# Second MoE of an attention + MoE + MoE kernel: token blocks of 256, 512, 512, 512 in place of seven of 256, and products of 512 and 384 columns

## The chip, the cores and the metric

One core of one Trainium2 chip runs the kernel. Times are device microseconds (us). The metric is the time of one execution. The kernel before took 1158.94 us in the median of 3 runs (1152.77 to 1166.38). A further execution was profiled, and the rows below come from it.

## The reference

Three stages run one after the other, all in float32:

```python
q_n, k_n = rmsnorm(q, g_q), rmsnorm(k, g_k)          # q, k, v: (4, 12, 448, 64)
attn = softmax(q_n @ k_n^T / 8);  x = attn @ v       # then to x: (1792 tokens, 768)
h = x @ w_in; s = h * softmax(h); x = (layernorm(s) * g_ln) @ w_out      # 768 -> 1024 -> 768
h = x @ w2_in; g = h - tanh(h);   out = g @ w2_out                       # 768 -> 2048 -> 768
```

The weights of both MoE stages come as 64-bit floats, and the kernel converts them on the chip.

## The kernel before

**Numbers.** Every operand of a product is split into a high part (float32r, what TensorE multiplies in one pass) and a low part (the remainder). A product of two split operands is three matmuls into the same PSUM buffer: high by high, high by low, low by high. That is `three` (L174 to L177), so the matmuls of all stages carry the lines L175, L176 and L177, and the tile names tell them apart. `split` (L179 to L181) makes a high part on ScalarE (L180) and the low part on VectorE (L181).

**Stages.** Attention runs over pairs of heads. The first MoE runs over four blocks of tokens (384, 384, 384 and 384+256), one block behind the attention that feeds it: `x_split` loads and splits tokens (tiles xr, xs), `moe_h` multiplies by w_in (hps), `layer_norm` works on the rows (hb), `moe_lnT` transposes them on TensorE (lps) and splits them (lnT), and `moe_x2` multiplies by w_out (x2ps), copies the result to SBUF (x2) and writes it to a DRAM buffer, x2d. The last block's `moe_h` and `moe_x2` run when attention is over.

**The second MoE** goes over 8 spans of 256 hidden columns, and in each span over the token blocks, 7 of 256. `h2(sp, i)` (L785) multiplies block i by the span's input weights: the weights stand still, 256 tokens move, 36 matmuls into one PSUM buffer h2ps (pool ps_h, 5 buffers). Tanh on ScalarE (L797), h - tanh(h) on VectorE (L798) and a split follow (tile gT, 2 buffers). `out2(sp, i)` (L803) takes gT as the standing operand and 256 columns of the output weights as the moving one: three PSUM buffers ops (pool ps_m, 3 buffers) of 12 matmuls, each then added by VectorE to the block's sum in SBUF, ob (L820; in the first span ScalarE copies it, L818). `out2` of a block is written after `h2` of the next.

**Tokens of the second MoE.** `x2_load(i)` (L775) reads block i back from x2d with one DMA and splits it in two halves (tiles x2s): two ScalarE instructions, then two VectorE ones. Blocks 0 and 1 are loaded before the first MoE's last block is finished, so that their `h2` can fill TensorE's waits there. The other five have buffers only when the first MoE's pools are closed (L836, L837).

**Weights of the second MoE.** `Stream.convert` (L116) turns one raw tile of 64-bit floats into a split weight: one GpSimd instruction (L131), four on VectorE (L132, L133, L137, L140), one on ScalarE (L153), one on GpSimd (L154). A span needs three tiles of w2_in (kind in2) and three of w2_out (out2). There are 4 buffers for them before the first MoE ends and 9 after.

**Order.** A scheduler puts each engine's instructions in a fixed order when the program is built, by its own cost estimates. Each engine then works through its list strictly in that order, and an instruction whose input is late holds up all behind it on that engine. All DMAs are issued by SyncE (SP), whose list is as strict.

Of the kernel before, what the change touches and what calls it, by code (L numbers as in the profile page):

```python
# [18 lines left out]
def kernel(  # L19
# [24 lines left out]
    TB = 256  # L44
    NB = NTOK // TB
# [49 lines left out]
    class Stream:  # L95
# [20 lines left out]
        def convert(self, kind, i, pool, save):  # L116
# [3 lines left out]
            w = pool.tile([128, 2, a, b], F32R, tag="w6", name="w6")  # L120
# [39 lines left out]
        def conv(self, n):  # L160
            while self.nc < min(n, len(self.items)):
                self.load(self.nc + 1)
                kind, i, again = self.items[self.nc]
                if again:
                    a, b = source(kind, i)[1]
                    w = self.pool().tile([128, 2, a, b], F32R, tag="w6", name="w6")
                    nc.sync.dma_start(out=w.bitcast(F32), in_=saved[kind, i])
                else:
                    w = self.convert(kind, i, self.pool(), self.save)
                self.got[self.nc] = w  # L170
                self.nc += 1
                self.load(self.nc + 2)
# [356 lines left out]
    Bp = {}  # L529
# [171 lines left out]
    ws = Stream(items, lambda: Bp["w"], True)  # L701
# [49 lines left out]
    def open_c(side, sizes):  # L751
        for name, bufs in sizes:
            C.setdefault(name, []).extend(
                [ec.enter_context(tc.tile_pool(name=f"c_{name}_{side}", bufs=bufs, side=side))] * bufs
            )

    CI, CW = 2, 4
    open_c("right", (("w", CW), ("xh", 2 * CI), ("ob", CI), ("g", 2), ("th", 2)))
# [3 lines left out]
    n_w = [0]  # L762

    def next_w():
        n_w[0] += 1
        return C["w"][(n_w[0] - 1) % len(C["w"])]
# [8 lines left out]
    def x2_load(i):  # L775
        x2 = C["ob"][i].tile([128, KD, TB], F32, tag="x", name="x2")
        nc.sync.dma_start(out=x2, in_=x2d[:, :, TB * i:TB * i + TB])
        pr = []
        for z in range(2):
            s = C["xh"][2 * i + z].tile([128, 2, 3, TB], F32R, tag="xh", name="x2s")  # L780
            split(s[:, 0], s[:, 1], x2[:, 3 * z:3 * z + 3])
            pr.append(s)
        xs_t.append(pr)

    def h2(sp, i):  # L785
        ps = ps_h.tile([128, 2, TB], F32, tag="h", name="h2ps")
# [16 lines left out]
    def out2(sp, i, G):  # L803
        if sp == 0:
            ob[i] = C["ob"][i].tile([128, 2, DM], F32, tag="x", name="ob")
        for th in range(DM // 256):
            ps = ps_m.tile([128, 2, 256], F32, tag="m", name="ops")
            for t in range(2):
                for f in range(2):
                    w = w2.got[6 * sp + 3 + th]  # L810
                    cols = slice(128 * t, 128 * t + 128)
                    three(
                        ps[:, t], (G[:, 0, f, cols], G[:, 1, f, cols]), (w[:, 0, f], w[:, 1, f]),
                        f == 0, f == 1,
                    )
            o = ob[i][:, :, 256 * th:256 * th + 256]
            if sp == 0:
                nc.scalar.activation(out=o, in_=ps, func=AF.Copy)  # L818
            else:
                nc.vector.tensor_tensor(out=o, in0=ps, in1=o, op=ALU.add)  # L820
            if sp == NSP - 1 and i == NB - 1:
                nc.sync.dma_start(
                    out=out[TB * i:TB * i + TB, 256 * th:256 * th + 256].rearrange("(t p) d -> p t d", p=128), in_=o
                )
        if sp == NSP - 1 and i < NB - 1:
            nc.sync.dma_start(
                out=out[TB * i:TB * i + TB, :].rearrange("(t p) d -> p t d", p=128), in_=ob[i]
            )

    w2.conv(CW)  # L830
    for i in range(CI):
        x2_load(i)
# [4 lines left out]
    open_c("left", (("w", 5), ("xh", 2 * (NB - CI)), ("ob", NB - CI)))  # L837
    prev = None
    for sp in range(NSP):
        for i in range(NB):  # L840
            if sp == 0 and i >= CI:
# [44 lines left out]
```

## Time and profile before

| what | value |
|---|---|
| median of 3 runs | 1158.94 us (1152.77 to 1166.38) |
| the profiled execution, its own time | 1158.77 us |
| its span, first to last instruction | 1156.9 us |
| TensorE (PE) busy | 93% of the span |
| VectorE (DVE), ScalarE (ACT), GpSimd (POOL) busy | 64%, 45%, 23% |
| granted TensorE clock, mean | 0.976 of full speed |

The span is 1.9 us shorter than the execution's time. In the rows, PE is TensorE's matmul side and PEld its weight load; a matmul's own duration includes its way through the array, so matmuls overlap, and what one costs in a stream is the distance from one start to the next.

### The profile page before, as it was taken

To read this page: it belongs to the slowest core of one execution; us is meant where nothing else is said; L and a number is where in the kernel's file an instruction comes from. 1 tells how busy PE (TensorE), PEld (TensorE's weight loads), DVE (VectorE), ACT (ScalarE), POOL (GpSimd) and SP (SyncE) were. 2 spreads that over 40 slices of the span, in tenths; PEclk is the share of its full clock that TensorE was granted. 3 is DMA by queue.
4 is the path that set the end of the run, shared out by engine and by line. 5 is a ranking of instruction groups with operands and counts; after the bars stand their busy time and mean duration, and the time that the engine had idled before them with its cause. 6 is when DMAs were issued, how large, how long until landed. Compare 5 with 4: busy or idle time off the path is not lost.

```text
span 1156.9 us, 19235 instructions
## 1 busy us (share of the span) xinstructions
PE 1071.2 (93%) x7152; PEld 948.0 (82%) x7152; DVE 740.8 (64%) x1331; ACT 525.3 (45%) x1064; POOL 263.5 (23%) x228
## 2 busy tenths in 40 slices
PE   5989988969887989997999999999999999999998
PEld 3545566646776779776998999999999999999998
DVE  8566677699798866654527045558575757667434
ACT  5466666688676767665226145312121212122111
POOL 3211122222312411111201031416050414142100
PEclk9999999998999899998999999999999999999999
DMA  6776688776997877765737534112121111211022
GB/s 173 204 220 170 169 220 230 217 216 208 266 290 239 251 207 212 194 210 165 247 110 227 181 125 137 60 52 74 38 74 38 56 56 46 65 37 56 1 83 110
DMA packets 112893, 171.53 MB, mean 148 GB/s; under 512 B 33328, under 2 KB 79136, under 8 KB 112800
## 3 DMA queue, kind: packets, MB, share of 16 engines
q1 hardware_dynamic: 112800, 170.30, 50.2%
q8 instruction: 57, 0.93, 0.3%
q14 instruction: 36, 0.29, 0.1%
HBM read 109.41 MB, written 29.20 MB: 120 GB/s over the span
## 4 chain that ended last, share of the span: by engine, by line
PE 66%; DMA 15%; DVE 9%; ACT 5%; issue 2%; SPq 1%; POOL 0%; DVEq 0%; ACTq 0%; POOLq 0%
PE ops L177 7%; PE h2ps L176 7%; PE h2ps L175 7%; PE h2ps L177 7%; PE ops L176 7%; PE ops L175 7%; PE pvps L440 5%; PE sps L393 3%; PE hps L175 2%; DMA w<-w_in 2%; DMA raw<-in_moe_w_out_dram 2%; PE x2ps L175 2%; PE hps L177 2%; PE hps L176 2%; PE x2ps L177 2%; PE x2ps L176 2%
## 5 line engine op out<-in xcount | busy, mean ns | idle before, releaser
L175 PE MATMUL ops<-w,gT 128*128 128x256 f32 x672 | 189.6, 282 | 1.4 <-ACT ob L818 0.8
L176 PE MATMUL h2ps<-x2s,w 128*128 128x256 f32 x672 | 189.5, 282 | 0.0
L176 PE MATMUL ops<-w,gT 128*128 128x256 f32 x672 | 189.4, 282 | 0.0
L177 PE MATMUL ops<-w,gT 128*128 128x256 f32 x672 | 188.9, 283 | 0.5 <-DVE gT L181 0.5
L177 PE MATMUL h2ps<-x2s,w 128*128 128x256 f32 x672 | 189.3, 282 | 0.0
L175 PE MATMUL h2ps<-x2s,w 128*128 128x256 f32 x672 | 189.3, 282 | 0.0
L154 POOL TENSOR_TENSOR w<-val,w 128x512 fp32r<-128x512 f32 x60 | 80.5, 1351 | 388.2 <-ACT w L153 382.1
L355 DVE TENSOR_REDUCE nm<-mps 128x1 f32<-128x448 f32 x168 | 103.1, 619 | 79.7 <-PE mps L354 73.7
L393 PE MATMUL sps<-q,k 128*128 128x448 f32 (+1 forms) x368 | 120.0, 415 | 23.0 <-DVE nm L355 9.4
L175 PEld LDWEIGHTS ops<-w,gT 128*128 128x128 f32 x672 | 127.7, 190 | 2.0 <-ACT ob L818 1.2
L176 PEld LDWEIGHTS ops<-w,gT 128*128 128x128 f32 x672 | 127.6, 190 | 0.0
L177 PEld LDWEIGHTS ops<-w,gT 128*128 128x128 f32 x672 | 126.8, 189 | 0.7 <-DVE gT L181 0.7
L175 PEld LDWEIGHTS h2ps<-x2s,w 128*128 128x128 f32 x672 | 127.2, 189 | 0.1
L177 PEld LDWEIGHTS h2ps<-x2s,w 128*128 128x128 f32 x672 | 127.0, 189 | 0.0
L176 PEld LDWEIGHTS h2ps<-x2s,w 128*128 128x128 f32 x672 | 126.9, 189 | 0.0
L798 DVE TENSOR_TENSOR th<-h2ps,th 128x512 f32<-128x512 f32 x56 | 38.6, 689 | 134.4 <-ACT th L797 134.4
L820 DVE TENSOR_TENSOR ob<-ops,ob 128x512 f32<-128x512 f32 x147 | 100.4, 687 | 24.5 <-PE ops L177 20.2
L797 ACT ACTIVATE th<-h2ps 128x512 f32<-128x512 f32 x56 | 33.4, 596 | 171.9 <-PE h2ps L177 171.3
L404 ACT ACTIVATE pf<-sps 128x448 f32<-128x448 f32 x167 | 87.6, 539 | 50.5 <-PE sps L393 42.5
L393 PEld LDWEIGHTS sps<-q,k 128*128 128x128 f32 (+1 forms) x368 | 63.5, 187 | 55.3 <-DVE nm L355 16.6
L175 PE MATMUL hps<-w,xs 128*128 128x256 f32 x336 | 97.4, 291 | 6.2 <-DMA w<-w_in 5.7
L176 PE MATMUL hps<-w,xs 128*128 128x256 f32 x336 | 95.9, 286 | 0.0
(139 smaller groups left out, 2371.2 us busy)
## 6 DMA issues: line engine op xcount, KB each, us to landing
w<-w_out SPq DMA_DIRECT2D x48, 512.0 KB
raw<-in_moe_w_in_dram SPq DMA_DIRECT2D x36, 512.0 KB
raw<-in_moe_w_out_dram SPq DMA_DIRECT2D x36, 512.0 KB
w<-w_in SPq DMA_DIRECT2D x36, 512.0 KB
q<-wq SPq DMA_DIRECT2D x138, 112.0 KB
k<-wk SPq DMA_DIRECT2D x46, 224.0 KB
w_in<-w SPq DMA_DIRECT2D x12, 512.0 KB
w_out<-w SPq DMA_DIRECT2D x12, 512.0 KB
```

The source lines that it names most:

```text
L154: nc.gpsimd.tensor_tensor(out=w[:, 1], in0=x, in1=w[:, 0].bitcast(F32), op=ALU.subtract)
L175: nc.tensor.matmul(ps, lhsT=a[0], rhs=w[0], start=first, stop=False)
L176: nc.tensor.matmul(ps, lhsT=a[0], rhs=w[1], start=False, stop=False)
L177: nc.tensor.matmul(ps, lhsT=a[1], rhs=w[0], start=False, stop=last)
L355: nc.vector.tensor_reduce(out=nm_t[p][:, c:c + 1], in_=ps, axis=AX.X, op=ALU.max, negate=True)
L393: nc.tensor.matmul(o, lhsT=K[p % NQ][:, i, z, k0:k0 + m], rhs=Q[p % 2][:, i, z], start=(z == 0), stop=(z == 1))
L404: nc.scalar.activation(out=x, in_=ps, func=AF.Exp)
L440: nc.tensor.matmul(o, lhsT=w, rhs=x, start=first, stop=last)
L797: nc.scalar.activation(out=th, in_=ps, func=AF.Tanh)
L798: nc.vector.tensor_tensor(out=th, in0=ps, in1=th, op=ALU.subtract)
L820: nc.vector.tensor_tensor(out=o, in0=ps, in1=o, op=ALU.add)
```

## The change

- The second MoE's blocks are (first token, tokens) = (0, 256), (256, 512), (768, 512), (1280, 512).
- `h2` works with up to 512 moving columns: one PSUM buffer per half span (18 matmuls each), and tanh, subtraction and split per half.
- `out2` works by 128 tokens with 384 moving columns: 6 matmuls per PSUM buffer, still 3 buffers.
- The three out2 weight tiles of a span lie side by side in one wide tile (w18). Pools for weights: in2 4 buffers early and 1 later, wide out2 tiles 1 early and 1 later. Six weight tiles, not four, are converted before the first MoE's last stages.
- Only block 0 is loaded early. Block 1 gets buffers (xh1, ob1) at the bottom of the left stack, and the first MoE's pools are put in another order so that the ones used up first (xs, xr, hb) lie there.

```diff
-    TB = 256
-    NB = NTOK // TB
+    blocks2 = [(0, 256), (256, 512), (768, 512), (1280, 512)]
+    NB = len(blocks2)
...
-        ("xs", 1), ("lnT", 1), ("xr", 2), ("hb", 3), ("one", 1), ("x2", 2), ("small", 4), ("w", 4), ("wp", 1),
+        ("xs", 1), ("xr", 2), ("hb", 3), ("one", 1), ("wp", 1), ("lnT", 1), ("x2", 2), ("small", 4), ("w", 4),
...
-    CI, CW = 2, 4
-    open_c("right", (("w", CW), ("xh", 2 * CI), ("ob", CI), ("g", 2), ("th", 2)))
+    open_c("right", (("wi", 4), ("wo", 1), ("xh0", 2), ("ob0", 1), ("g", 2), ("th", 2)))
...
     def h2(sp, i):
-        ps = ps_h.tile([128, 2, TB], F32, tag="h", name="h2ps")
+        T = blocks2[i][1]
+        G = C["g"][0].tile([128, 2, 2, T], F32R, tag="g", name="gT")
         for s in range(2):
+            ps = ps_h.tile([128, T], F32, tag="h", name="h2ps")
             for c in range(KD):
...
-        th = C["th"][0].tile([128, 2, TB], F32, tag="th", name="th")
-        nc.scalar.activation(out=th, in_=ps, func=AF.Tanh)
-        nc.vector.tensor_tensor(out=th, in0=ps, in1=th, op=ALU.subtract)
-        G = C["g"][0].tile([128, 2, 2, TB], F32R, tag="g", name="gT")
-        split(G[:, 0], G[:, 1], th)
+            th = C["th"][0].tile([128, T], F32, tag="th", name="th")
+            nc.scalar.activation(out=th, in_=ps, func=AF.Tanh)
+            nc.vector.tensor_tensor(out=th, in0=ps, in1=th, op=ALU.subtract)
+            split(G[:, 0, s], G[:, 1, s], th)
...
     def out2(sp, i, G):
-        for th in range(DM // 256):
-            ps = ps_m.tile([128, 2, 256], F32, tag="m", name="ops")
+        w = w2.got[6 * sp + 3]
+        for t in range(T // 128):
+            rows = slice(128 * t, 128 * t + 128)
+            for d in range(0, DM, 384):
+                ps = ps_m.tile([128, 384], F32, tag="m", name="ops")
                 for f in range(2):
...
-    w2.conv(CW)
-    for i in range(CI):
-        x2_load(i)
+    w2.conv(6)
+    x2_load(0)
...
-    open_c("left", (("w", 5), ("xh", 2 * (NB - CI)), ("ob", NB - CI)))
+    open_c("left", (("xh1", 2), ("ob1", 1), ("xh", 2 * (NB - 2)), ("wi", 1)))
+    open_c("right", (("ob", NB - 2), ("wo", 1)))
...
-            if i == 0:
-                w2.conv(6 * sp + 6)
-            if i in (3, 4, 5):
-                w2.conv(6 * sp + 4 + i)
             if prev is not None:
                 out2(*prev)
+            w2.conv(6 * sp + (7, 9, 11, 12)[i])
```

The line numbers of the changed kernel are 7 higher from L160 on (8 to 10 in the second MoE): L132 becomes L139, L181 becomes L188, L820 becomes L830.

Each engine's list is the same in both kernels up to the point where attention ends; from there on the scheduler has ordered it anew. On SP, at that point, before (x2_6212 is block 1's token tile, xo the last attention result, xd and x2d the DRAM buffers between stages, w_in_0 a weight tile of the first MoE):

```order
L638 DMA x2d_70<-x2_6079 128x384
L777 DMA x2_6212<-x2d_70 128x6x256
L472 DMA xd_71<-xo_6104 128x448
L538 DMA xr_6229<-xd_71 128x2x384
L538 DMA xr_6234<-xd_71 128x2x256
L167 DMA w6_6349<-w_in_0_1412 128x1024
```

and on SP at the same point now:

```order
L645 DMA x2d_70<-x2_6079 128x384
L479 DMA xd_71<-xo_6104 128x448
L545 DMA xr_6244<-xd_71 128x2x384
L545 DMA xr_6249<-xd_71 128x2x256
L174 DMA w6_6364<-w_in_0_1412 128x1024
```

The read of block 1's tokens no longer stands between two writes of results; it comes some 40 rows later, as one read of 512 tokens.

On DVE, at the same point of the program, before (x2s is block 1's split, lnT the split of the first MoE's transposes lps):

```order
L469 TENSOR_TENSOR sx_6046<-sx_6046,xo_6104 128x448
L470 TENSOR_TENSOR xu_6047<-xu_6047,xo_6104 128x448
L181 TENSOR_TENSOR x2s_6214<-x2_6212,x2s_6214 128x768
L181 TENSOR_TENSOR x2s_6217<-x2_6212,x2s_6217 128x768
L471 SCALAR_TENSOR_TENSOR xo_6104<-sx_6046,xu_6047 128x448
L181 TENSOR_TENSOR lnT_6246<-lps_6275,lnT_6246 128x4x128
L181 TENSOR_TENSOR lnT_6246<-lps_6282,lnT_6246 128x4x128
```

and on DVE now:

```order
L476 TENSOR_TENSOR sx_6046<-sx_6046,xo_6104 128x448
L477 TENSOR_TENSOR xu_6047<-xu_6047,xo_6104 128x448
L188 TENSOR_TENSOR lnT_6261<-lps_6290,lnT_6261 128x4x128
L478 SCALAR_TENSOR_TENSOR xo_6104<-sx_6046,xu_6047 128x448
L188 TENSOR_TENSOR lnT_6261<-lps_6297,lnT_6261 128x4x128
```

The two x2s instructions of block 1 are gone from between xu and xo.

On DVE in a later span of the second MoE, where `out2` of the third block meets `h2` of the next span's first, now (ops are the PSUM buffers that the adds empty, val the steps of a weight's conversion):

```order
L830 TENSOR_TENSOR ob_7860<-ops_8846,ob_7860 128x384
L140 TENSOR_SCALAR val_9121<-val_9121 128x512
L808 TENSOR_TENSOR th_8924<-h2ps_8905,th_8924 128x256
L144 SCALAR_TENSOR_TENSOR val_9121<-raw64_9026,val_9121 128x512
L830 TENSOR_TENSOR ob_7860<-ops_8854,ob_7860 128x384
L147 SCALAR_TENSOR_TENSOR val_9121<-raw64_9026,val_9121 128x512
L139 SCALAR_TENSOR_TENSOR val_9245<-raw64_9118,val_9245 128x512
L830 TENSOR_TENSOR ob_7860<-ops_8862,ob_7860 128x384
L140 TENSOR_SCALAR val_9245<-val_9245 128x512
L830 TENSOR_TENSOR ob_7860<-ops_8870,ob_7860 128x384
```

and on DVE before, at a comparable place of a span:

```order
L820 TENSOR_TENSOR ob_8194<-ops_8870,ob_8194 128x2x256
L132 SCALAR_TENSOR_TENSOR val_9208<-raw64_8854,val_9208 128x512
L820 TENSOR_TENSOR ob_8194<-ops_8884,ob_8194 128x2x256
L133 TENSOR_SCALAR val_9208<-val_9208 128x512
L137 SCALAR_TENSOR_TENSOR val_9208<-raw64_8854,val_9208 128x512
L140 SCALAR_TENSOR_TENSOR val_9208<-raw64_8854,val_9208 128x512
L132 SCALAR_TENSOR_TENSOR val_9304<-raw64_9120,val_9304 128x512
```

Adds and conversion steps alternate as before; the adds are smaller and there are 224 of these PSUM buffers in place of 168.

## Rows read from the trace of the kernel before

**Rows 1.** Page: its first line (span and instructions).
```profile
span 1156.9 us, 19235 instructions
```
**Rows 2.** Table by stretch: start:end, us, then busy us of each engine (instructions), PEclk, DMA share, GB/s.
```profile
531.00:540.00 9.00, 5.59 (x35) 4.30 (x36) 4.15 (x6) 7.24 (x13) 0.00 (x0) 0.97 0.57 195
540.00:547.00 7.00, 2.42 (x8) 1.62 (x7) 4.79 (x8) 3.70 (x6) 0.91 (x1) 0.50 0.30 108
559.00:612.00 53.00, 52.28 (x427) 51.80 (x428) 19.12 (x37) 12.32 (x29) 5.09 (x4) 1.00 0.50 170
676.00:706.00 30.00, 28.13 (x227) 27.27 (x226) 23.74 (x30) 15.99 (x27) 13.92 (x9) 1.00 0.62 198
760.00:1060.00 300.00, 300.00 (x2510) 300.00 (x2509) 202.24 (x297) 61.03 (x101) 89.63 (x60) 1.00 0.18 55
```
**Rows 3.** PE's instructions in order of time (start us, us, what): x2ps, 650 to 660.
```profile
652.03 0.28 PE L175 MATMUL x2ps<-lnT,w 128*128 128x256 f32 x1
...
654.83 0.34 PE L175 MATMUL x2ps<-lnT,w 128*128 128x384 f32 x1
...
659.06 0.28 PE L175 MATMUL x2ps<-lnT,w 128*128 128x256 f32 x1
```
**Rows 4.** The same view, attention's last products of 448 columns.
```profile
532.63 0.37 PE L440 MATMUL pvps<-ph,vl 128*128 128x448 f32 x1
...
534.04 0.36 PE L440 MATMUL pvps<-pl,va 128*128 128x448 f32 x1
```
**Rows 5.** The same view: PE after a wait (in brackets idle us and releaser), 534 to 685.
```profile
539.02 1.71 PE L623 MATMUL lps<-idf,hb 128*128 128x128 f32 x8 [3.41 <-DVE lnT L181]
544.22 0.69 PE L175 MATMUL x2ps<-lnT,w 128*128 128x384 f32 x1 [3.49 <-ACT lnT L180]
546.00 0.69 PE L176 MATMUL x2ps<-lnT,w 128*128 128x384 f32 x1 [1.09 <-DVE lnT L181]
...
559.24 0.39 PE L175 MATMUL hps<-w,xs 128*128 128x256 f32 x1 [0.62 <-DMA w<-w_in]
...
684.34 0.39 PE L175 MATMUL ops<-w,gT 128*128 128x256 f32 x1 [0.83 <-ACT ob L818]
```
**Rows 6.** The chain that ended last (start us, us, what), 526 to 562.
```profile
531.24 6.02 DMA x2d<-x
...
537.28 4.80 DMA x<-x2d
...
545.38 1.95 DMA xd<-xo
...
548.05 4.08 DMA xr<-xd
...
554.31 4.89 DMA w<-w_in
```
**Rows 7.** DVE's instructions in order of time, 540 to 546.
```profile
540.61 0.62 DVE L470 TENSOR_TENSOR xu<-xu,xo 128x448 f32<-128x448 f32 x1
542.99 1.83 DVE L181 TENSOR_TENSOR x2s<-x,x2s 128x768 fp32r<-128x768 f32 x2 [1.75 <-ACT x2s L180]
544.73 0.62 DVE L471 SCALAR_TENSOR_TENSOR xo<-sx,xu 128x448 f32<-128x448 f32 x1
```
**Rows 8.** Groups of DVE by line and form, 700 to 1157: busy us, mean ns | idle before.
```profile
L820 DVE TENSOR_TENSOR ob<-ops,ob 128x512 f32<-128x512 f32 x147 | 100.4, 687 | 24.5 <-PE ops L177 20.2
L181 DVE TENSOR_TENSOR gT<-th,gT 128x512 fp32r<-128x512 f32 x53 | 39.8, 751 | 4.9 <-ACT gT L180 4.8
L132 DVE SCALAR_TENSOR_TENSOR val<-raw,val 128x512 f32<-128x512 f32 x38 | 37.6, 989 | 7.8 <-POOL val L131 7.8
L798 DVE TENSOR_TENSOR th<-h2ps,th 128x512 f32<-128x512 f32 x52 | 35.9, 689 | 131.7 <-ACT th L797 131.7
L137 DVE SCALAR_TENSOR_TENSOR val<-raw,val 128x512 int32<-128x512 int32 x38 | 31.6, 831 | 0.8
L140 DVE SCALAR_TENSOR_TENSOR val<-raw,val 128x512 int32<-128x512 int32 x38 | 26.0, 685 | 0.7
L133 DVE TENSOR_SCALAR val<-val 128x512 int32<-128x512 int32 x38 | 16.6, 437 | 0.4
```

More of the change, by code (lines that the diff above doesn't have):

```diff
@@ L119, in convert @@
             a, b = t.shape[1:3]
-            w = pool.tile([128, 2, a, b], F32R, tag="w6", name="w6")
+            if kind == "out2":
+                if i % 3 == 0:
+                    self.wide = pool.tile([128, 2, a, 3 * b], F32R, tag="w18", name="w18")
+                w = self.wide[:, :, :, b * (i % 3):b * (i % 3) + b]
+            else:
+                w = pool.tile([128, 2, a, b], F32R, tag="w6", name="w6")
             val = raw_p.tile([128, a, b], I32, tag="val", name="val")
@@ L165, in conv @@
                     a, b = source(kind, i)[1]
-                    w = self.pool().tile([128, 2, a, b], F32R, tag="w6", name="w6")
+                    w = self.pool(kind, i).tile([128, 2, a, b], F32R, tag="w6", name="w6")
                     nc.sync.dma_start(out=w.bitcast(F32), in_=saved[kind, i])
                 else:
-                    w = self.convert(kind, i, self.pool(), self.save)
-                self.got[self.nc] = w
+                    w = self.convert(kind, i, self.pool(kind, i), self.save)
+                self.got[self.nc] = self.wide if kind == "out2" else w
                 self.nc += 1
@@ L761, with next_w @@
     ps_h = ec.enter_context(tc.tile_pool(name="c_ps_h", bufs=5, space=PSUM))
[L762 to L766, printed above, removed]
+    def next_w(kind, i):
+        sp, r = divmod(i, 3)
+        pools = C["wi"] if kind == "in2" else C["wo"]
+        return pools[(3 * sp + r if kind == "in2" else sp) % len(pools)]
     items = []
@@ L775, in x2_load @@
     def x2_load(i):
-        x2 = C["ob"][i].tile([128, KD, TB], F32, tag="x", name="x2")
-        nc.sync.dma_start(out=x2, in_=x2d[:, :, TB * i:TB * i + TB])
+        t0, T = blocks2[i]
+        z0 = str(i) if i < 2 else ""
+        x2 = C["ob" + z0][0].tile([128, KD, T], F32, tag="x", name="x2")
+        nc.sync.dma_start(out=x2, in_=x2d[:, :, t0:t0 + T])
         pr = []
         for z in range(2):
-            s = C["xh"][2 * i + z].tile([128, 2, 3, TB], F32R, tag="xh", name="x2s")
+            s = C["xh" + z0][0].tile([128, 2, 3, T], F32R, tag="xh", name="x2s")
             split(s[:, 0], s[:, 1], x2[:, 3 * z:3 * z + 3])
@@ L814, in out2 @@
                         f == 0, f == 1,
                     )
[L816 to L824, printed above, removed]
@@ L825, in out2 @@
-        if sp == NSP - 1 and i < NB - 1:
-            nc.sync.dma_start(
-                out=out[TB * i:TB * i + TB, :].rearrange("(t p) d -> p t d", p=128), in_=ob[i]
-            )
-    w2.conv(CW)
-    for i in range(CI):
-        x2_load(i)
+                o = ob[i][:, t, d:d + 384]
+                if sp == 0:
+                    nc.scalar.activation(out=o, in_=ps, func=AF.Copy)
+                else:
+                    nc.vector.tensor_tensor(out=o, in0=ps, in1=o, op=ALU.add)
+                if sp == NSP - 1 and i == NB - 1:
+                    nc.sync.dma_start(out=out[t0 + 128 * t:t0 + 128 * t + 128, d:d + 384], in_=o)
@@ L833 @@
+        if sp == NSP - 1 and i < NB - 1:
+            nc.sync.dma_start(out=out[t0:t0 + T, :].rearrange("(t p) d -> p t d", p=128), in_=ob[i])
+    w2.conv(6)
+    x2_load(0)
     while b <= NBK:
@@ L840 @@
         for i in range(NB):
[L841 removed]
+            if sp == 0 and i >= 1:
                 x2_load(i)
             G = h2(sp, i)
[L844 to L847 removed]
             if prev is not None:
                 out2(*prev)
+            w2.conv(6 * sp + (7, 9, 11, 12)[i])
             prev = (sp, i, G)
```

14 lines of the change are left out of this document (6 added, 8 removed).

## Prediction

> **What bounds the kernel now.** I read the table by stretch first, since the share of PE over the whole span hides stages with different limits. From 760 to 1060 us PE is busy all of the 300 us, while DVE works 202 and ACT 61 of them (the engines stand in the order PE, PEld, DVE, ACT, POOL) [rows 2]. There the second MoE is bound by the matmuls alone: an edit counts if it changes what a matmul costs, or if it makes PE wait. PE waits in three places around the change: at the end of attention, 3.41 us of 531 to 540 and 4.58 of 540 to 547; 0.72 us in 559 to 612, the last block's `moe_h`; and 1.87 us in 676 to 706, the hand-over to the second MoE [rows 2]. What each waits for stands in brackets in PE's instructions in order of time [rows 5], and the chain that ended last leads back from there [rows 6]. The sum below is made against the profiled execution, 1158.77 us, of which the span is 1156.9 [rows 1]; the median of 1158.94 lies 0.17 above it.
>
> **A: the matmuls of the second MoE.** Before, 8 spans x 7 blocks x 72 matmuls make 4032, all of 256 columns. Now `h2` has 36 of 256 and 3 x 36 of 512 per span (288 and 864), `out2` 14 groups of 128 tokens x 2 x 6 = 168 of 384 (1344): 2496 matmuls. The columns are the same, 1,032,192 in all, so only a price per matmul can be saved.
> Prices. 2510 matmuls in 300 us, two of them begun before, are 0.1196 us each at 256 columns [rows 2]. In `moe_x2` 24 matmuls of 256 take 652.03 to 654.83, 0.1167 each, and 24 of 384 take 654.83 to 659.06, 0.1763 each [rows 3]. The step of 128 columns costs 0.0596, so a straight line gives 0.2359 at 512; 0.1763 taken per column gives 0.2350, which I use. Seven distances of 448 columns from 532.63 to 534.04 are 0.2014 each [rows 4]; per column that makes 0.230 at 512.
> Before: 4032 x 0.1196 = 482.2. Now: 288 x 0.1196 + 864 x 0.235 + 1344 x 0.1763 = 34.4 + 203.0 + 236.9 = 474.4, a gain of 7.8. But a matmul of 256 costs 0.0029 more in the second MoE than in `moe_x2`, and nothing shows whether a wide one does too. If all 2208 wide ones do, 6.4 is lost again; if the cost follows columns alone, the gain is 0; with 0.230 at 512 it is 11.8. I take a quarter of the extra, 1.6: **-6.2** (-11.8 to 0).
> The trace has the 256-column matmul at 119.6 ns and the 384-column one at 176.3, a price that is nearly all columns. The Trainium skill, "TensorE: Matmul & The Clock Gate", section "Back-to-back issue gap", gives for a warm array the columns over 2.4 GHz and some 2.5 ns for each matmul, 109 and 162.5 ns; by it 1536 matmuls fewer would give back 3.8 us, an estimate, in place of 6.2. The trace disagrees with the size, by 10.6 and 13.8 ns for one matmul.
>
> **B: the end of attention.** On SP the load of block 1's tokens (x from x2d) stands before the write of the last attention result (xd from xo), and on DVE its two splits x2s stand between xu and xo. That load starts when the write before it has landed, 531.24 + 6.02, takes 4.80, ACT's half of the split follows, then DVE's two in 1.83, and only at 544.73 comes xo, which ends at 545.35 [rows 6, 7]. From there the chain goes on by xd 1.95, xr 4.08 and a weight of 4.89 to hps at 559.24 [rows 5, 6]. Now xu ends at 541.23, one lnT follows and then xo, at 0.62 [rows 7]; for lnT I take as much as for xo, and the end is near 542.4, 3.0 earlier. The same two x2s hold up the lnT for which x2ps waits 3.49 and 1.09 [rows 5], so PE gets the 3.0 too. Block 0's load keeps its place and with it the wait of 3.41. In this stretch the granted clock is 0.50, the level of 1.2 GHz [rows 2]; an earlier end of the waits may shorten that a little. The wait of 0.62 before hps I expect half gone. **-3.3** (-4.5, nearly all of the 4.58 that PE waits in 540 to 547, to -1, if the next write or read is late in its place).
>
> **C: fewer fillers under `moe_h`.** In 559 to 612 the first MoE's weights come as raw tiles, and PE's list fills the waits for them with `h2` of blocks 0 and 1: 72 matmuls before, 36 now, since block 1 is not there. PE waits 0.72 in this stretch with them [rows 2]. If every matmul missing became a wait, it would be 36 x 0.1196 = 4.3; the work itself is only moved to after the hand-over, so its time is in A. Two more weights of the second MoE are also read early and share the queue. The DMAs are busy half of the stretch [rows 2] and the earlier end of B doesn't bring the weights sooner; I take a third, **+1.5** (0 to 4.3).
>
> **D: the hand-over.** Five blocks wait for buffers there; PE waits 1.87 in 30 us, 0.83 of it for ACT's copies ob [rows 2, 5]. Now block 1 sits at the bottom of the stack, its buffers are free early, and when the pools close PE has its `h2` (36 x 0.235 = 8.5) and block 0's `out2` (18 x 0.1763 = 3.2), 11.7 us of work, before block 2 is needed. Block 2 needs the last write to x2d, up to 6.0 as the write of rows 6, then one read of twice the tokens, 4.80 to 9.6, and a split of 1.3 or so per half: at worst 16.9, that is 5.2 late. The DMAs are no emptier there (0.62) [rows 2]. Half of the present wait is gone, I take: **-1.0** (-1.9 to +5.2).
>
> **E: VectorE and three PSUM buffers.** An ops buffer now holds 6 x 0.1763 = 1.06 us of matmuls, not 12 x 0.1196 = 1.44, and there are still three: an add may come late by the two other buffers, 2.12 now, 2.87 before. In the steady stage DVE works 202 of 300 us [rows 2], and an add of 512 columns takes 0.687 [rows 8]. One of 384 takes 0.515 by columns and 0.687 at most; I take 0.55. Over a span the change is small: 28 adds x 0.55 = 15.4 in place of 21 x 0.687 = 14.4. What counts is the densest stretch of a span, the third block's `out2` beside the next span's first `h2` (its order on DVE is shown with the change). PE has 8 x 1.06 + 36 x 0.12 = 12.8 us of work there. DVE's list has 8 adds (4.4), two conversions and two steps of another (2 x 2.94, from 0.989 + 0.437 + 0.831 + 0.685, and 0.831 + 0.685: 7.4), th once at 0.689 and twice at half size, for which I take 0.4 (1.5), and gT likewise from 0.751 (1.55) [rows 8]: 14.85. That is 2.05 more than PE's work and just within the cover of 2.12. Each instruction's own duration may be longer than its share of a back-to-back stream, so 2.05 is more likely too high than too low. If the cover were gone, 7 spans would pay 2.05 each, 14.4. I take **+1.0** (0 to 14.4).
>
> **F: the end.** The last add before the output is of 384 columns in place of 512, and the last DMA has fewer tokens' columns behind it: **-0.2** (-0.4 to +0.3), by the difference of 0.687 and 0.515.
>
> Sum: -6.2 - 3.3 + 1.5 - 1.0 + 1.0 - 0.2 = -8.2; 1158.8 - 8.2 = **1150.6 us**.
>
> **Rivals.**
> *Columns alone decide (A = 0, the rest small).* For it: 384 costs 0.1763 where 256 costs 0.1167, 1.511 times as much for 1.5 times the columns [rows 3], so in the nearest pair of rows nothing at all is saved, and the whole of A hangs on the 0.0029 by which the second MoE's 256 are dearer. Against it: the row of 448 is 0.450 per column, under both [rows 4]. With A = 0 and the rest as above: 1158.8 - 2.0 = 1156.8.
> *More is given back.* If 512 columns go at the price per column of [rows 4] and wide matmuls have none of the extra, A is -11.8; with B -3.8, C +0.5, D -1.9, E 0 and F -0.2 the sum is -17.2: 1141.6. For it: the 2.9 ns look like a price of each matmul in a stream with many weight changes; the wait in D is only needed for blocks that are not there. Against it: each term must be good at once.
> *VectorE cannot empty the buffers (slower).* In the dense stretch of each span PE then waits for the add that frees an ops buffer, as `L820` would be named before an ops matmul. For it: 14.85 of work against 12.8, and a shorter cover; the conversions are in the same list and an add behind one waits for it. Against it: the table shows PE with no wait at all in 300 us [rows 2], DVE is idle a third of that time, and th's 131.7 us of idle time before L798 [rows 8] is slack that other instructions could use. The time turns above that of before when the other terms (-9.2) are used up, at 1.3 us a span; at the full 2.05 it is 1158.8 - 9.2 + 14.4 = 1164.0, and with 3 us a span 1170.6.
>
> **How the numbers follow.** The forecast has 0.44, the larger gain 0.25, columns alone 0.18, VectorE 0.13. The range from 1139 (the larger gain, 2.6 below its sum) to 1165 (just past VectorE's 1164.0) leaves out the upper part of the VectorE case and what lies below the larger gain, some 0.15 together; the likeliest case alone has 1145 to 1156. A measurement of this kernel can tell about 1% from no change, that is a time under 1147.3 or above 1170.5. Faster by over 1% are most of the larger gain (0.23) and the lower end of the forecast (0.14): 0.37. Slower by over 1% is the worse half of the VectorE case and a stall that none of my rows shows: 0.11. The rest, 0.52, lies within 1%.
>
> **What would show each step right or wrong.** A: the distance between matmuls of 512 columns in a full stretch, 0.235, and of 384, 0.176; below 0.230 the larger gain is on, above 0.239 columns alone. If the steady stage is still 100% busy, eight spans shrink by 6.2 together. B: xo's write begins some 3 us earlier than 545.38, and hps too. C: PE's idle time between the first hps and the last; over 4 us makes the step wrong. D: a wait for a DMA before block 2's `h2` above 1.9 us. E: ops matmuls that wait for L830; more than 1.3 us a span would turn the sign. A stretch of waits in the second MoE in which the granted clock falls to 0.50 would make the whole sum wrong, as would a first MoE that takes longer before attention ends, where both lists agree.

## The result, and the profile after

The changed kernel took 1141.65 us in the median of 4 runs (1140.80 to 1144.83), the kernel before 1159.39 beside it; the ratio is 0.986, with an interval of 0.982 to 0.990. Two further sets of runs of the same kernel, told below, gave medians of 1143.70 and 1142.94. The forecast was 1150.6 with a range of 1139 to 1165: the sign is right and the time lies in the range, but the gain is twice the forecast one and stands where the rival "more is given back" put it (1141.6).

The page's first line, of the changed kernel:

```profile
span 1139.0 us, 16212 instructions
```

It answers to [rows 1]: 17.9 us shorter, with 3023 instructions fewer. The table by stretch of the changed kernel has the columns of [rows 2]: start:end, us, busy us of PE, PEld, DVE, ACT and POOL (instructions), granted clock, DMA share, GB/s.

```profile
531.00:540.00 9.00, 5.10 (x29) 3.93 (x27) 5.70 (x9) 7.46 (x13) 0.00 (x0) 0.87 0.28 106
540.00:547.00 7.00, 6.81 (x28) 6.81 (x29) 2.39 (x5) 2.04 (x4) 5.50 (x4) 0.68 0.53 166
559.00:612.00 53.00, 50.14 (x386) 48.66 (x385) 31.52 (x68) 17.27 (x39) 14.37 (x10) 1.00 0.61 206
676.00:706.00 30.00, 30.00 (x148) 26.58 (x148) 20.86 (x26) 16.88 (x28) 12.62 (x8) 1.00 0.32 107
760.00:1060.00 300.00, 300.00 (x1590) 274.74 (x1589) 200.33 (x340) 64.42 (x113) 88.94 (x60) 1.00 0.16 48
```

Against [rows 2] the 4.58 us of waiting in 540 to 547 have become 0.19, and the 1.87 of the hand-over are gone. The 2.86 us that PE is idle in 559 to 612 can't be held against the 0.72 of before: here `moe_h` ends at 601, and the stretch takes in 11 us of what follows. The steady stage is as full as it was, now with 1590 matmuls in 300 us. What PE waits for between 525 and 700 us is in the view of waits (engine and line, what it waited for: us in total, times, longest):

```profile
PE lps L630 <- DVE lnT L188: 5.5, 4, 3.4
PE hps L182 <- DMA w<-w_in: 2.6, 4, 1.3
PE x2ps L183 <- DVE lnT L188: 0.7, 1, 0.7
PE x2ps L182 <- DMA w<-w_out: 0.3, 1, 0.3
```

The wait of 3.4 for lnT is that of [rows 5], unchanged; the 3.49 and 1.09 before x2ps [rows 5] have become 0.7. Under `moe_h` the waits for weights have grown from 1.1, which the same view has for the kernel before, to 2.6:

```profile
PE hps L175 <- DMA w<-w_in: 1.1, 3, 0.6
```

**Where the time went.** Attention, which both kernels work through by the same lists, ends at another time in every execution: its last product began between 527.9 and 550.1 us in the profiles of this study. So I cut the program at five matmuls, the last of attention (pvps), the first and the last of the last `moe_h` (hps), the last of `moe_x2` (x2ps) and the last of `out2` (ops), and compare what lies between. They are read from PE's instructions in order of time, here of the kernel before (its last pvps, 534.04, is in [rows 4]):

```profile
556.04 0.28 PE L175 MATMUL hps<-w,xs 128*128 128x256 f32 x1
...
608.78 0.28 PE L177 MATMUL hps<-w,xs 128*128 128x256 f32 x1
...
675.79 0.28 PE L177 MATMUL x2ps<-lnT,w 128*128 128x256 f32 x1
...
1152.60 0.28 PE L177 MATMUL ops<-w,gT 128*128 128x256 f32 x1
```

and of the changed kernel:

```profile
532.35 0.36 PE L447 MATMUL pvps<-pl,va 128*128 128x448 f32 x1
...
550.50 0.28 PE L182 MATMUL hps<-w,xs 128*128 128x256 f32 x1
...
600.98 0.28 PE L184 MATMUL hps<-w,xs 128*128 128x256 f32 x1
...
669.17 0.28 PE L184 MATMUL x2ps<-lnT,w 128*128 128x256 f32 x1
...
1135.10 0.34 PE L184 MATMUL ops<-w,gT 128*128 128x384 f32 x1
```

| step, us | before | after | difference |
|---|---|---|---|
| last pvps to first hps (end of attention) | 22.00 | 18.15 | -3.85 |
| first to last hps (`moe_h`, with fillers) | 52.75 | 50.48 | -2.27 |
| to the last x2ps (transposes, `moe_x2`) | 67.01 | 68.19 | +1.18 |
| to the last ops (second MoE) | 476.80 | 465.93 | -10.87 |
| to the end of the span | 4.3 | 3.9 | -0.4 |
| all behind attention | 622.9 | 606.6 | -16.2 |

The other 1.7 us of the two spans' difference lie before the last pvps, where nothing was changed. Of the fillers 36 matmuls have moved to the fourth row, 4.3 us: 32 from the second row (3.8) and 4, which stood behind the last hps, from the third (0.5). So `moe_h` has in truth lost 1.6, the transposes and `moe_x2` have lost 1.7, and the second MoE has gained 15.2.

**The price of a matmul** now, in PE's instructions in order of time:

```profile
802.39 0.39 PE L183 MATMUL h2ps<-x2s,w 128*128 128x512 f32 x1
...
807.52 0.40 PE L184 MATMUL h2ps<-x2s,w 128*128 128x512 f32 x1
807.76 0.34 PE L182 MATMUL ops<-w,gT 128*128 128x384 f32 x1
...
810.89 0.39 PE L182 MATMUL h2ps<-x2s,w 128*128 128x512 f32 x1
```

From 802.39 to 807.76 there are 23 distances of 512 columns, 0.2335 each, and from there to 810.89 18 distances of 384, 0.1739 each. Over 730 to 1130 us the 1158 distances of 384 columns have a mean of 0.1747 and the 738 of 512 one of 0.2331; a distance of 256 columns is 0.1185 here (216 of them) and 0.1196 in the same stretch of the kernel before, 0.1194 in `h2` and 0.1198 in `out2`.

### The profile page after: what moved, and what is told of

It reads as the page before. It is cut to its first block, busy times and chain, and to the rows that moved or that the text cites. A ratio compares the mean times of both kernels' runs of the same rounds, so it can differ in the third digit from the quotient of the medians.

```text
span 1139.0 us, 16212 instructions
## 1 busy us (share of the span) xinstructions
PE 1058.6 (93%) x5616; PEld 897.0 (79%) x5616; DVE 739.4 (65%) x1390; ACT 529.2 (46%) x1081; POOL 264.0 (23%) x228
## 4 chain that ended last, share of the span: by engine, by line
PE 63%; DMA 19%; DVE 8%; ACT 5%; SPq 3%; issue 2%; POOL 1%; ACTq 0%; DVEq 0%; POOLq 0%
PE ops L183 7%; PE ops L184 7%; PE ops L182 7%; PE h2ps L183 7%; PE h2ps L184 7%; PE h2ps L182 7%; PE pvps L447 4%; DMA raw<-in_moe_w_in_dram 4%; PE sps L400 3%; DMA raw<-in_moe_w_out_dram 3%; DMA m<-nt 3%; PE x2ps L182 2%; PE x2ps L184 2%; PE x2ps L183 2%; DMA w<-w_in 2%
## 5 line engine op out<-in xcount | busy, mean ns | idle before, releaser
L830 DVE TENSOR_TENSOR ob<-ops,ob 128x384 f32<-128x384 f32 x196 | 108.5, 554 | 104.1 <-PE ops L184 103.5
L183 PE MATMUL ops<-w,gT 128*128 128x384 f32 x448 | 150.5, 336 | 0.0
L182 PE MATMUL ops<-w,gT 128*128 128x384 f32 x448 | 150.3, 336 | 0.0
L184 PE MATMUL ops<-w,gT 128*128 128x384 f32 x448 | 150.2, 335 | 0.0
L183 PE MATMUL h2ps<-x2s,w 128*128 128x512 f32 (+1 forms) x384 | 140.8, 367 | 0.0
L184 PE MATMUL h2ps<-x2s,w 128*128 128x512 f32 (+1 forms) x384 | 140.7, 367 | 0.0
L182 PE MATMUL h2ps<-x2s,w 128*128 128x512 f32 (+1 forms) x384 | 140.4, 366 | 0.0
L807 ACT ACTIVATE th<-h2ps 128x512 f32<-128x512 f32 (+1 forms) x64 | 34.9, 545 | 182.2 <-PE h2ps L184 181.9
L400 PEld LDWEIGHTS sps<-q,k 128*128 128x128 f32 (+1 forms) x368 | 65.1, 191 | 52.7 <-DVE nm L362 16.2
L182 PE MATMUL hps<-w,xs 128*128 128x256 f32 x336 | 98.6, 294 | 7.3 <-DMA w<-w_in 6.3
L183 PE MATMUL hps<-w,xs 128*128 128x256 f32 x336 | 96.9, 289 | 0.0
L184 PE MATMUL hps<-w,xs 128*128 128x256 f32 x336 | 96.3, 287 | 0.3 <-DVE xs L188 0.3
L139 DVE SCALAR_TENSOR_TENSOR val<-raw,val 128x512 f32<-128x512 f32 x48 | 44.0, 917 | 69.5 <-POOL val L138 69.3
L183 PEld LDWEIGHTS ops<-w,gT 128*128 128x128 f32 x448 | 84.2, 188 | 4.6
L182 PEld LDWEIGHTS ops<-w,gT 128*128 128x128 f32 x448 | 84.2, 188 | 4.4
L361 PE MATMUL mps<-k,q 128*128 128x448 f32 (+1 forms) x144 | 69.0, 486 | 18.9 <-DMA q<-wq 5.3
L138 POOL TENSOR_SCALAR val<-raw 128x512 f32<-128x512 f32 x48 | 78.8, 1644 | 32.9 <-DMA raw<-in_moe_w_out_dram 14.2
L182 PE MATMUL x2ps<-lnT,w 128*128 128x384 f32 (+1 forms) x240 | 82.4, 344 | 2.0 <-DMA w<-w_out 1.8
```

The lines of the kernel that those rows point to most:

```text
L138: nc.gpsimd.tensor_scalar(out=fv, in0=fh, scalar1=2.0 ** -15, scalar2=None, op0=ALU.max)
L139: nc.vector.scalar_tensor_tensor(out=fv, in0=fh, scalar=-1.0, in1=fv, op0=ALU.mult, op1=ALU.max)
L182: nc.tensor.matmul(ps, lhsT=a[0], rhs=w[0], start=first, stop=False)
L183: nc.tensor.matmul(ps, lhsT=a[0], rhs=w[1], start=False, stop=False)
L184: nc.tensor.matmul(ps, lhsT=a[1], rhs=w[0], start=False, stop=last)
L361: nc.tensor.matmul(ps, lhsT=qh.rearrange("p c q -> p (c q)")[:, f:f + 128], rhs=kh, start=True, stop=True)
```

## The experiments

### The changed kernel again, twice

Nothing is edited.

> The changed kernel once more, nothing edited, on the chip of the other two. Theory: what the change gave lies behind attention's last product, 622.9 us before and 606.6 now, and will repeat within 1 us (606 to 607.5); attention itself ends anywhere from 531 to 540 us in the profiles so far although both lists agree there, so the whole time may come out 2 to 5 us above the first four runs, about 1143 to 1147. Rival, the first runs show the true gain of 17.5: a median of 1141 to 1143 beside the same 1159.

> The changed kernel a third time, nothing edited, beside the other one on the same chip. Theory: the step from the last x2ps to the last ops is 465.9 again and the time behind attention 606 to 607.5; the median of the runs lies between 1140 and 1146, by where attention ends.

Medians 1143.70 (ratio 0.983, interval 0.976 to 0.990) and 1142.94 (0.986, 0.981 to 0.990). The last pvps began at 537.53 and 537.26, the time behind it was 606.9 and 606.2, and the step of the second MoE 465.94 in both. So the time behind attention repeats within 0.7 us, and the spans of the three profiles (1139.0 to 1144.5) differ by where attention ends. Whole runs scatter more: the six of the first set lie between 1128.6 and 1146.3. A difference of a few us is to be read from the steps, and that is how the following runs are compared.

### Each product at its old width

`h2` alone:

```diff
-            for c in range(KD):
+            for t in range(0, T, 256):
+                for c in range(KD):
...
-                    ps, (w[:, 0, c % 2, cols], w[:, 1, c % 2, cols]),
-                    (xs[:, 0, c % 3], xs[:, 1, c % 3]), c == 0, c == KD - 1,
+                        ps[:, t:t + 256], (w[:, 0, c % 2, cols], w[:, 1, c % 2, cols]),
+                        (xs[:, 0, c % 3, t:t + 256], xs[:, 1, c % 3, t:t + 256]), c == 0, c == KD - 1,
```

> The changed kernel with every h2 product of 512 columns made as two of 256 (the same buffers, halves, tanh and splits). Theory, a price per matmul: 864 matmuls at 0.2333 us become 1728 at 0.1196, 201.6 to 206.7 us, so the span of 1139.0 grows by about 5.1 to 1144. Rival, columns alone: the 256-column ones would go at 0.1167 and the span would stay within 0.5 of 1139. The distance between two 256-column matmuls in the steady stage tells, 0.1196 or 0.1167, and it should be free of the noise of whole runs.

`out2` alone:

```diff
-            for d in range(0, DM, 384):
-                ps = ps_m.tile([128, 384], F32, tag="m", name="ops")
+            for d in range(0, DM, 256):
+                ps = ps_m.tile([128, 2, 256], F32, tag="m", name="ops")
...
-                o = ob[i][:, t, d:d + 384]
+                o = ob[i][:, t:t + 2, d:d + 256]
```

> The changed kernel with out2 as before: 256 moving columns, 12 matmuls and 512 columns in a PSUM buffer; h2 keeps 512. Theory, a price per matmul: 1344 at 0.1747 us become 2016 at 0.1196, 234.8 to 241.1 us, span 1139.0 to about 1145.3. Rival, columns alone: 2016 at 0.1167, 235.2, no change. Rival, smaller adds cost something on VectorE: then a part of the 6.3 would come back as fewer waits; as PE waits nowhere in the steady stage I expect none.

The second MoE took 471.37 with narrow `h2`, 5.43 more than 465.94, and 472.67 with narrow `out2`, 6.73 more. PE waited nowhere in it in either. The table by stretch of the first, and then of the second:

```profile
760.00:1060.00 300.00, 300.00 (x2118) 300.00 (x2118) 192.96 (x343) 64.44 (x112) 82.91 (x60) 1.00 0.16 50
```

```profile
760.00:1060.00 300.00, 300.00 (x2007) 276.16 (x2006) 194.96 (x303) 62.79 (x110) 86.85 (x59) 1.00 0.16 48
```

Over 730 to 1130 us a 256-column matmul cost 0.1194 in the narrow `h2` and 0.1197 in the narrow `out2` (mean distance), not the 0.1167 of [rows 3]. The two parts make 12.2 us together, expected were 5.1 and 6.3. Both rivals fall: the cost does not go with columns alone, and the larger adds of the old form bring nothing back. What isn't separated is whether the price is one of the matmul or of its weight load: each matmul of these kernels has a load of its own, and with 256 columns in `h2` PEld is busy all of the 300 us (300.00 above, 274.74 in the changed kernel). Whole runs (medians 1152.51 and 1152.14, ratios 0.993 and 0.995) have the sign; attention ended 8 and 2 us later in these two profiles than in the first one of the changed kernel.

### The kernel before with only block 0 loaded early

```diff
-    CI, CW = 2, 4
+    CI, CW = 1, 4
```

> The kernel before with block 0 alone loaded early (pools for one block; nothing else). Theory: the step from the lps wait to the first hps shrinks from 17.0 us (539.02 to 556.04) to about 13.2 as in the changed kernel, the waits of PE under the last moe_h grow from 1.2 to about 3 us because 36 fillers are gone, and at the hand-over PE has only block 0's out2 (36 x 0.12 = 4.3 us) before block 1 is needed, whose read and split take some 10 us: 5 to 8 us of waiting in place of 1.9. Whole span about 1156.9 - 3.8 + 1.9 + 5 = 1160. Rival, the early load of block 1 costs nothing at attention's end: that step stays at 17 and the span is about 1164.

The end of attention took 17.82, 4.2 less than before, by this edit alone: one early load in place of two is enough for it. The edit doesn't show block 1's load by itself, for the scheduler also issued block 0's read later, 0.43 us behind the last pvps in place of 7.55 ahead of it, and the wait of 3.41 became 1.43. `moe_h` took 53.19 with 34 of the 36 lost fillers missing in it, so it lost 4.5, more than expected: its waits were 3.9 in place of 1.1, and behind the longest of them (2.13) the granted clock was 0.50 for 3.4 us, some 1.7 more. At the hand-over PE stood still for the split of block 1, in PE's order of time and the table by stretch:

```profile
678.29 0.38 PE L175 MATMUL h2ps<-x2s,w 128*128 128x256 f32 x1 [2.42 <-ACT x2s L180]
679.28 0.39 PE L176 MATMUL h2ps<-x2s,w 128*128 128x256 f32 x1 [0.61 <-DVE x2s L181]
```

```profile
671.00:701.00 30.00, 25.54 (x192) 24.52 (x191) 23.93 (x30) 13.71 (x23) 14.01 (x10) 0.94 0.61 194
```

The second MoE took 485.54, 8.74 more than before: 4.3 of work moved there, 2.6 of waiting (4.5 in place of 1.9), and in these 30 us a granted clock of 0.94, worth 1.8. Whole runs: 1163.88, ratio 1.003 (1.000 to 1.006). Giving up the early load pays only where something takes its place at the hand-over.

### The changed kernel with block 1 on top of the stack

```diff
-    open_c("left", (("xh1", 2), ("ob1", 1), ("xh", 2 * (NB - 2)), ("wi", 1)))
+    open_c("left", (("xh", 2 * (NB - 2)), ("wi", 1), ("xh1", 2), ("ob1", 1)))
```

> The changed kernel with block 1's buffers at the top of the left stack, blocks 2 and 3 below, so that block 1's read waits for the first MoE's last pools. Theory: PE has block 0's out2 alone (18 x 0.1747 = 3.1 us) while the read (7 us) and the first half of the split (3) go on: 6 to 9 us of waiting near 672 to 680, span about 1146. Rival, another order fills the gap (transposes, the last x2ps moved behind) and the new place of block 1 was worth nothing: span within 1 us of 1139.

The end of attention (17.87) and `moe_h` (50.86) stay, the second MoE takes 473.81, 7.87 more. PE's order of time and the table by stretch show the price:

```profile
684.19 1.22 PE L182 MATMUL h2ps<-x2s,w 128*128 128x512 f32 x2 [4.67 <-ACT x2s L187]
685.98 0.80 PE L183 MATMUL h2ps<-x2s,w 128*128 128x512 f32 x1 [0.57 <-DVE x2s L188]
```

```profile
675.00:705.00 30.00, 24.76 (x106) 20.16 (x105) 20.34 (x24) 16.03 (x21) 8.46 (x6) 0.89 0.55 197
```

5.24 us are waits, and the granted clock of the stretch is 0.89: behind the longer wait PE works for a while at the level of 1.2 GHz. The place of block 1's buffers alone is worth 7.9 us. Median 1154.31, ratio 0.996 (0.994 to 0.997).

### Two ops buffers in place of three, and a control

```diff
-    ps_h = ec.enter_context(tc.tile_pool(name="c_ps_h", bufs=5, space=PSUM))
+    ps_h = ec.enter_context(tc.tile_pool(name="c_ps_h", bufs=3, space=PSUM))
+    ps_o = ec.enter_context(tc.tile_pool(name="c_ps_o", bufs=2, space=PSUM))
...
-                ps = ps_m.tile([128, 384], F32, tag="m", name="ops")
+                ps = ps_o.tile([128, 384], F32, tag="m", name="ops")
```

> The changed kernel with two PSUM buffers for ops in place of three (a pool of their own; h2ps has 3 in place of 5 to make room). The cover behind a late add falls from 2.12 us to 1.06. Theory: VectorE was never late by more than one buffer, so two are nearly enough: the step from the last x2ps to the last ops grows by 0 to 4 us over 465.9. Rival (the slower case of the prediction): the dense stretch of each span runs 2 us behind, then two buffers cost 1 us or more a span, 8 to 15 us in all, with ops matmuls waiting for the adds of L830 (its line number here may differ by one or two).

The control has the first edit alone (ps_h 3, ops in their three buffers of ps_m):

> The control to the run with two ops buffers: ops keep their three, h2ps has three in place of five. Theory: the 36.6 us that the step from the last x2ps to the last ops grew there (502.5 against 465.9) come from the ops buffers, 20.5 of its 24.7 us of waits stand before ops; with three of them the step is back within 466 to 470. Rival, the two h2ps buffers that were taken away made the order and the waits: the step stays above 485.

With two buffers the second MoE took 502.54, 36.6 more; the control 465.94, no different, with PE's and DVE's lists in the same order as in the changed kernel. So it is the ops buffers, and what the rival expected (8 to 15 us) was too little. But with two buffers the scheduler also ordered both lists anew, with up to 30 ops matmuls in a row where the changed kernel has at most 18; the 36.6 are the price of both together. In the changed kernel's own order the third buffer is needed too: of its 224 ops buffers 28 were emptied later than the start of the second group of ops after them, by up to 2.3 us, but all of them at least 0.96 us ahead of the start of the third. The table by stretch and the waits of PE in it, with two buffers:

```profile
760.00:1060.00 300.00, 279.67 (x1418) 251.29 (x1417) 190.41 (x313) 52.63 (x98) 86.05 (x56) 0.96 0.18 53
```

```profile
PE ops L182 <- DVE ob L831: 20.3, 12, 3.2
```

24.7 us of the 36.6 are waits of PE in the whole stage; the clock of 0.96 in these 300 us is worth another 12, an estimate (300 x 0.04). How one such wait comes about is in the order of time of DVE and of PE there:

```profile
774.30 1.74 DVE L139 SCALAR_TENSOR_TENSOR val<-raw,val 128x512 f32<-128x512 f32 x1 [1.71 <-POOL val L138]
775.96 0.55 DVE L831 TENSOR_TENSOR ob<-ops,ob 128x384 f32<-128x384 f32 x1
```

```profile
776.56 0.64 PE L182 MATMUL ops<-w,gT 128*128 128x384 f32 x1 [3.18 <-DVE ob L831]
777.00 0.52 PE L183 MATMUL ops<-w,gT 128*128 128x384 f32 x1
777.32 0.52 PE L184 MATMUL ops<-w,gT 128*128 128x384 f32 x1
```

VectorE sits 1.71 us in front of a conversion step (L139) that waits for GpSimd, the step takes 1.74, and the add behind it in the list, which would free the buffer, comes 3.5 us late. Behind the wait the matmuls of 384 columns start 0.32 apart, not 0.174. (This kernel's line 831 is 830 of the changed one.) Median 1178.54, ratio 1.019 (1.013 to 1.025).

### Block 0's load off the end of attention, two ways

On GpSimd:

```diff
+            if i == 0:
+                nc.gpsimd.tensor_copy(out=s[:, 0], in_=x2[:, 3 * z:3 * z + 3])
+                nc.gpsimd.tensor_tensor(out=s[:, 1], in0=x2[:, 3 * z:3 * z + 3], in1=s[:, 0].bitcast(F32), op=ALU.subtract)
+            else:
+                split(s[:, 0], s[:, 1], x2[:, 3 * z:3 * z + 3])
```

> The changed kernel with the split of block 0's tokens (both parts, four instructions) on GpSimd, which is idle from 527 to 541 us there, in place of ScalarE and VectorE. Theory: as for block 1, the two x2s on VectorE stand ahead of the lnT for which PE waits 3.41 us at the end of attention; without them the first lnT can run at about 534.6 in place of 536.6, and the step from the last attention product to the first hps falls from 18.15 to about 16 us, the time behind attention from 606.6 to about 604.5. Rival, the lnT waits for something else there (ScalarE's own list, lps buffers) and the step stays within 0.5 of 18.15; or GpSimd's four instructions (2 to 2.5 us each) come too late for the fillers of the last moe_h and the gain is lost there.

The wait of 3.41 fell to 1.43 + 0.30, but the step to the first hps stayed at 18.39: a new wait of 2.16 before x2ps took its place. PE's order of time, and then GpSimd's and VectorE's:

```profile
538.44 0.69 PE L183 MATMUL x2ps<-lnT,w 128*128 128x384 f32 x1 [2.16 <-DVE lnT L188]
```

```profile
533.17 3.60 POOL L791 TENSOR_TENSOR x2s<-x,x2s 128x768 fp32r<-128x768 f32 x2
...
535.59 1.67 DVE L476 TENSOR_TENSOR sx<-sx,xo 128x448 f32<-128x448 f32 x1
...
537.17 0.61 DVE L477 TENSOR_TENSOR xu<-xu,xo 128x448 f32<-128x448 f32 x1
```

The sx step of the changed kernel:

```profile
538.39 0.61 DVE L476 TENSOR_TENSOR sx<-sx,xo 128x448 f32<-128x448 f32 x1
```

The sx step, 0.61 there, took 1.67 beside GpSimd's subtraction, and all behind it on VectorE came 1.06 later. That is the difference to the next run, which has the same 1.43 + 0.30 without GpSimd's part: there the wait before x2ps is 1.11. The Trainium skill, "SBUF — State Buffer", section "Terms", says that VectorE and GpSimd share a pair of ports which one of them holds for a whole instruction while the other is blocked; the row agrees: sx is 1.06 us longer and ends 0.49 behind GpSimd's two subtractions. `moe_h` took 52.98, 2.3 more than in the three profiles of the changed kernel (mean 50.69), with 5.3 us of waits for weights in it, so that all behind attention took 609.0, 2.4 more. The median of the whole runs was 1143.67, beside 1143.70 for the changed kernel.

Through the first MoE's xr buffers, behind the last block's reads:

```diff
         if b < NBK:
             x_split(b)
+        if b == NBK - 1:
+            x2_load(0)
...
+            if i == 0:
+                xp = Bp["xr"].tile([128, 3, T], F32, tag="xr", name="xr")
+                nc.sync.dma_start(out=xp, in_=x2d[:, 3 * z:3 * z + 3, t0:t0 + T])
+                split(s[:, 0], s[:, 1], xp)
```

> The changed kernel with block 0's tokens read through the first MoE's xr buffers, behind the last block's own six reads: block 0's load and split leave the end of attention too, as block 1's did, and come under moe_h. Theory: the step from the last attention product to the first hps falls from 17.7 to 18.2 us in the changed kernel to about 16 (xo is no longer behind the x2s on ScalarE and VectorE, 1.6 us of ScalarE before xo); the fillers come later, so waits under moe_h may rise from 3 to 4. Whole time behind attention 606.7 to about 605.5, to be seen in the trace, hardly in whole runs. Rival, something else holds the end of attention (the transposes, the DMA of xd): the step stays within 0.4 of 17.9, and later fillers make the time the same or up to 2 us longer.

The step fell to 17.15, by 0.9 against the mean of the three profiles of the changed kernel (18.02), and `moe_h` rose to 55.29, by 4.6 (mean 50.69). The waits of PE between 545 and 640 us:

```profile
PE hps L182 <- DMA w<-w_in: 6.3, 2, 3.9
PE lps L630 <- DVE lnT L188: 1.7, 2, 1.4
PE x2ps L183 <- DVE lnT L188: 1.1, 1, 1.1
```

6.3 us for weights in place of 2.6: the fillers begin 33.3 us behind the last pvps, too late for the first of these waits (3.9 us, at 22.6). Behind attention it took 610.9 in all, 4.3 more than the changed kernel. This profile is of the longest of its ten runs (attention ends at 550.13), but the median of the ten points the same way: 1147.13, beside 1142.94 for the changed kernel, with intervals of the two ratios that overlap. Neither version beats the changed kernel: the 3.41 us wait can be removed, but what is gained before the first hps is lost at the weights behind it. The chains that ended last show one more reason, the write of the last attention result, in the changed kernel and then in these two:

```profile
540.69 2.01 DMA xd<-xo
```

```profile
539.55 3.91 DMA xd<-xo
```

```profile
557.44 3.83 DMA xd<-xo
```

It took 1.8 to 1.9 us longer in both, and the reads of xr and the next weights stand behind it in SP's list. Why it took longer the runs don't show.

## Why the prediction was right, and where its sum was wrong

**What bounds the kernel** held. The second MoE is bound by matmuls in both kernels, and the steps of the table account for the result: -3.85 - 2.27 + 1.18 - 10.87 - 0.4 = -16.2 behind attention, where the sum had -8.2.

**A was mis-sized: -6.2 was taken, -12.0 was measured, just outside its own range (-11.8 to 0).** Before, 4032 x 0.1196 = 482.2, as in the prediction. After, the step of 465.9 and the 36 fillers of 256 columns (4.3) make 470.2. Three of the term's prices were too high. 384 columns cost 0.1747, not the 0.1763 of the 24 distances in [rows 3], 2.2 us over 1344; 512 cost 0.2331, not 0.235, 1.6 over 864; and the quarter of the 2.9 ns extra, 1.6, does not exist, for the 384s are no dearer in the second MoE than in `moe_x2` (for 512 `moe_x2` has no row). The 256-column ones are, and the two runs at the old width show it is they: 0.1194 and 0.1197. The 288 that are left in the changed kernel cost 0.1185, another 0.3. The two parts undone one by one give 12.2. "Columns alone" is dead. The sign that the prediction set for A, a distance of 512 below 0.230 for the larger gain and 0.235 for the forecast, would not have told: 0.2331 lies between. Why a 256-column matmul costs 0.1185 to 0.1198 here and 0.1167 in `moe_x2` stays open.

By the rule of the Trainium skill, "TensorE: Matmul & The Clock Gate", section "Back-to-back issue gap", 1536 matmuls fewer would have given 3.8 us, an estimate; the runs have 12.0 to 12.2. Above the columns over 2.4 GHz they show 13 ns at 256, 15 at 384 and 20 at 512 columns where the rule has 2.5. The section calls the rule that of an isolated matmul, which the prediction did not say, and gives some 131 ns at 512 columns for a stream with weight loads; the stream here has 233.

**B held:** -3.3 was forecast, -3.85 measured, and the kernel before with one early load gives -4.2. The write of xo begins 8.34 us behind the last pvps in place of 11.34 (540.69 and 545.38), the 3.0 that the term took. The chain behind it acts on the first hps that waits for a weight, 25.2 us behind the last pvps before [rows 5] and 21.9 now:

```profile
554.29 0.39 PE L182 MATMUL hps<-w,xs 128*128 128x256 f32 x1 [0.18 <-DMA w<-w_in]
```

The first hps of all, by which the step is measured, is not released by it: PE goes into it from `moe_x2` without a wait in both kernels, and the step is 14.0 to 14.1 us of work and PE's waits for lnT, 7.99 before and 4.09 now. It is these that block 1's x2s held up.

**C held in sign and size:** +1.5 was forecast, +1.6 measured, and the waits for w_in grew by 1.5 (1.1 to 2.6 in the view of waits). Not foreseen is the +1.7 of the next step (1.2 and the four fillers), where the lps wait grew from 0.56 to 1.67 us: no term had it. The runs don't settle its cause, though all kernels here with one early block have it but the one whose ops had a pool of their own (0.55).

**D was too small:** -1.0 was forecast; all of the 1.87 went, and with what PE needs to start again it is some 3.0 (the eight distances at and behind the three waits of before make 3.96 us, where eight matmuls make 0.96). Block 2 is not late at all. What D rests on, the 11.7 us of work of block 1, is shown by the run that keeps it from being ready: +7.9. A, the 4.3 us of fillers and D make the -10.9 of the step within 0.2.

**E was 0, but for another reason than the one given.** The steady stage has no wait, as the main case had it (+1.0). The cover was put at 2.12 us, by ops matmuls alone. VectorE's list in the dense stretch of a span, in order of time:

```profile
764.86 0.69 DVE L139 SCALAR_TENSOR_TENSOR val<-raw,val 128x512 f32<-128x512 f32 x1
765.58 1.40 DVE L140 TENSOR_SCALAR val<-val 128x512 int32<-128x512 int32 x1
767.02 1.01 DVE L144 SCALAR_TENSOR_TENSOR val<-raw,val 128x512 int32<-128x512 int32 x1
...
768.55 0.54 DVE L830 TENSOR_TENSOR ob<-ops,ob 128x384 f32<-128x384 f32 x1
...
770.68 1.78 DVE L188 TENSOR_TENSOR gT<-th,gT 128x512 fp32r<-128x512 f32 x1
...
780.66 0.43 DVE L188 TENSOR_TENSOR gT<-th,gT 128x256 fp32r<-128x256 f32 x1
```

It works 16.2 us without a gap of over 0.15, with nine adds and three conversions where the sum's 14.85 had eight and two and a half, and single steps take up to 1.78. PE does not wait, for its list has h2ps matmuls after at most three groups of ops, so that a buffer is mostly needed later than 2.12 us on; the nearest comes 0.96 us after its add has ended. How near that is, the run with two buffers shows: 36.6 us, with the other order that goes with them. So the slower rival's mechanism and releaser are real, but with three buffers it does not start.

**F:** -0.2 forecast, -0.4 measured.

So the rival "more is given back" came nearest, in part by luck. The size of its A (-11.8) came, but not its price of 512 (0.230, measured 0.2331): cheaper 384s made up for it. Its B (-3.8) and E (0) came, its D (-1.9) was passed, its C (+0.5) did not come, and the +1.7 of the next step nobody had; and of the 17.9 us between the two spans 1.7 are of attention's end, which no edit moved. I had set it aside because every term had to be good at once; but A, B, D and E have causes that don't hang together with C, and in A the extra of 2.9 ns was given to wide matmuls with no row that showed it.

## What to carry to other kernels

Where TensorE has no idle time and the columns are fixed, the number of matmuls is still worth time: here 1536 fewer, each with its weight load, gave 12 of 482 us, and the price of each width is best taken from a few hundred distances of the stage itself. A load that is issued early for the sake of fillers is paid for in the lists it stands in: move it only if the work that it fed is replaced where it is missed next (here the same edit gave 0.986 with the buffers of block 1 freed early and 0.996 without). With few PSUM buffers look not at how busy the emptying engine is but at what stands ahead of each add in its list, and at what stands between the products in TensorE's.

## What the runs showed that was not expected

The second MoE's step is 465.94 us in six profiles, the three of the changed kernel, the control and the two with block 0 loaded otherwise, while attention, which no edit touched, ends anywhere in 22 us. One ops buffer fewer, with the order that the scheduler made for it, costs 36.6 us although VectorE is idle a third of the time, some third of it through the clock of TensorE behind the waits. And a VectorE instruction beside a GpSimd one took 1.67 us in place of 0.61.
